# A 32x128 score product issued as four 32x32 products in a two-branch attention kernel

## The chip, the cores and the metric

The kernel runs on one core of a Trainium2 chip. The metric is the device time of one execution in microseconds (us). The other seven cores are idle.

## What is computed

Two attention blocks over their own inputs, 2048 tokens, 1024 features, 32 heads of 32 features each; their outputs stand side by side. All data is bf16.

```
# A: full softmax attention
q, k, v = split(x @ wqkv)                       # 32 heads of 32
p = softmax(q @ k.T * 32**-0.5)                 # 2048 x 2048 per head
a = (p @ v) @ wo
# B: four segments of 512 tokens, causal inside a segment, with a memory M, z carried over
for s in range(4):
    p = softmax(qs @ ks.T * scale + mask)       # 512 x 512 per head
    a_dot = p @ vs
    a_mem = (phi(qs) @ M) / (phi(qs) @ z + 1e-6)
    o[s] = g * a_mem + (1 - g) * a_dot
    M += phi(ks).T @ vs;  z += sum(phi(ks))
b = o @ wo
out = concat(a, b, -1)
```

## The kernel before

Every step is recorded as an operation of one engine (class `Prog`, `op`), with the tiles that it reads and writes, a planned duration and a key. `schedule` then runs a list scheduler once, while the program is built, and fixes the order of the operations on each engine; `emit` writes that order out with the semaphore waits that the dependencies ask for. So the order on TensorE is written into the program, and each engine works through its own list in that order. The planned duration of a score set is `w / 2400.0 + 0.012` (L917); `SWITCH = 0.10` is planned where the shape of TensorE's tiles changes.

Scores are made transposed: 128 keys on the partitions, queries along the columns. A *set* (`plan_set`, L871) is four tiles of 128 keys by 512 columns, one for each of four heads. A head has 32 features, so a score product has 32 rows of contraction and 128 columns of stationary operand (the keys). The four heads of a set stand at rows 0, 32, 64 and 96 of the array and write to four different PSUM banks. For block A a tile has two pieces of 256 columns, so a set is eight products of 32 rows by 128 columns with 256 moving columns (L915). For block B a set has two or three pieces of 256 or 128 columns, eight or twelve products (`tiles_att_B`, L826). There are 512 sets of A (4096 products) and 80 of B (768 products).

PSUM has eight banks. Six of them make three slots of two banks (`SLOT_BANKS`, L23); a set takes two slots. Bank 6 is for the projections and other jobs, bank 7 for the attention output. ScalarE works one slot at a time: `plan_exp` (L963, activation at L994) takes the exponential of 128x1024 scores into the ring `P`. Of some sets of A one head's tile is not exponentiated by ScalarE but approximated by a cubic (`plan_cube`, L939): VectorE reads the scores (`Y`, L952), GpSimd works on them (`Z`, L955 and L956), and VectorE finishes (`Pc`, L957); ScalarE's activation of that slot is then 128x512.

TensorE has, beside the score sets, the products `P @ V` (L1090) and the row sums with a matrix of ones (L1097), and all projections by `mm4` (L551; the product is L556): four products of 128 rows by 32 columns side by side, writing to the four quarters of the partitions of one bank. So TensorE alternates between tiles of 128x32 and, for the score sets, tiles of 32x128. A score set waits until ScalarE has emptied the slots that it writes; an activation waits for the whole set, since only the last product of a set raises the semaphore.

The keys and queries of the score products lie in `KQ_A` and `KQ_B`, made by `proj_job` and copied out of PSUM by VectorE (L1248).

Of the kernel before, what the change touches and what calls it, by code (L numbers as in the profile page):

```python
# [72 lines left out]
def holds(rs, *tag):  # L73
    for r in rs:
        assert r.tag == tag, (r.tag, tag)
# [448 lines left out]
class _Kernel:  # L524
# [346 lines left out]
    def plan_set(self, take, T):  # L871
        w = take[0]["w"]
        slots = [(self.slot_n + k) % 3 for k in range(2)]
        n = self.slot_n + 1
        self.slot_n += 2
        banks = SLOT_BANKS[slots[0]] + SLOT_BANKS[slots[1]]
        kind = take[0]["kind"]
        cube = kind == "A" and take[0]["set"][3] in self.cubed(take[0]["unit"], take[0]["part"])
        bufs = [self.p_next(2 - (cube and not k)) for k in range(2)]
        for k, t in enumerate(take):  # L880
            t["n"] = n
            self.sets.setdefault(t["set"], []).append(t)
            if cube and not k:
                continue
            i = bufs[k // 2] + (0 if cube and k == 1 else k % 2)
            t["P"] = (self.Pt, i, self.r_P[i])

        def f(key):
            res = [self.bank[x] for x in banks]
            mms = []  # L890
            rd = []
            for p in range(len(take[0]["pieces"])):
                for b, t in enumerate(take):
                    kt, q, nq, off, g = t["pieces"][p]
                    h = t["h"]
                    rows = slice(32 * h, 32 * h + 32)
                    if kind == "A":
                        sl = g % 2
                        holds([r for x in self.r_KQA[sl] for r in x], "KQ", g)
                        kap = self.KQA[rows, sl, 0, P * kt:P * kt + P]  # L900
                        qap = self.KQA[rows, sl, 1, q:q + nq]
                        rd += [self.r_KQA[sl][0][kt // 4], self.r_KQA[sl][1][q // 512]]
                    else:
                        holds(self.r_KQB[g], "KQ", take[0]["s"], g)
                        kap = self.KQB[rows, g, 0, P * kt:P * kt + P]
                        qap = self.KQB[rows, g, 1, q:q + nq]
                        rd += [self.r_KQB[g][0], self.r_KQB[g][1]]
                    out = self.ps[:, 512 * banks[b] + off:512 * banks[b] + off + nq]
                    mms.append((out, kap, qap, h, p == 0))
            rd = list(dict.fromkeys(rd))  # L910

            def mm(e):
                ins = None
                for out, kap, qap, h, st in mms:
                    ins = e.matmul(out, kap, qap, start=st, stop=True, tile_position=(32 * h, 0), skip_group_check=True)  # L915
                return ins
            o = self.pe(mm, w / 2400.0 + 0.012, key - 1.5, rd, res, mode="row")  # L917
            o.urgent = True
            o.heat = 1.0
        self.item(T, f)  # L920
        T0 = T
        fix = self.fixes.pop(n - 1, None)
        if cube:
            self.fixes[n - 1 + CARRY - CARRY % 2] = self.plan_cube(take[0], banks[0], T)
        for k in range(2):
            lo = int(cube and not k)
            self.plan_exp(take[2 * k:2 * k + 2], slots[k], bufs[k], T, lo, fix if k == CARRY % 2 else None)
            T += (2 - lo) * w / 1200.0 + EXP_FIXED
        u = take[0]["unit"]
        self.st.setdefault(u, T0)  # L930
        self.en[u] = T
        if kind == "B":
            if take[0]["set"][3] == 2:
                self.st["B", u[1], u[2] + 1] = T0
            self.en["B", u[1], u[2] + 1] = T
        self.rounds.append((take, T, cube))
        return T
# [967 lines left out]
```

## Time and profile before

| | |
|---|---|
| times, three runs | 1124.29, 1128.17, 1129.32 us; median 1128.17 |
| the profiled execution, first to last instruction | 1128.2 us, equal to the median run; nothing is shown beside it |
| instructions | 67476, of them 31412 matmuls and 31412 weight loads |
| TensorE (PE) | busy 1045.6 us, 93% |
| ScalarE (ACT) | busy 1071.5 us, 95% |
| VectorE (DVE), GpSimd (POOL) | 744.9 us, 66%; 677.5 us, 60% |
| granted TensorE clock, mean | 0.996 |

How to read it: busy time is the time in which at least one instruction of the engine is under way. Matmuls are recorded with a modelled end, and several run beside each other in different tiles of the array, so the busy share of PE says how much of the time it had something, not how much of the array was used. In rows, `32*128 32x256` is a product with 32 rows and 128 columns of the array and a moving operand of 32 partitions by 256 columns. PEld is the weight load that goes ahead of each product. The chain is followed back from the last instruction, at each step to what released it or to the instruction before it on its engine.

### The profile page before, as it was taken

The page shows a single profiled execution, that of the slowest core. Times are in us where ns is not written, and L with a number is a line of the kernel's source. Part 1 is how long each engine was busy: PE and PEld are TensorE (multiplying, and loading weights), DVE is VectorE, ACT ScalarE, POOL GpSimd, SP SyncE. Part 2 cuts the span into 40 slices and gives each one's busy share as a digit, 9 for nine tenths or more (in the row PEclk, how much of TensorE's full clock was granted, in tenths as well). Part 3 has the DMA queues.
Part 4 walks back from the last instruction along what each step waited for, and adds up shares of the span by engine and source line. Part 5 has one row for each costly group of instructions (what it writes and reads, how often), then busy time and mean ns, then how long its engine had stood idle before and what let it go on. Part 6 is the DMA issues. An engine that isn't in the chain of part 4 may idle for free.

```text
span 1128.2 us, 67476 instructions
## 1 busy us (share of the span) xinstructions
PE 1045.6 (93%) x31412; PEld 724.2 (64%) x31412; DVE 744.9 (66%) x1566; ACT 1071.5 (95%) x1224; POOL 677.5 (60%) x653
## 2 busy tenths in 40 slices
PE   8989999999999988998999898988999889999998
PEld 4667666667666655666666566766667556657775
DVE  3345667756665588777865888687745868775444
ACT  4989999999999999999999999999999979999997
POOL 2215576756576576856565786775755758665431
PEclk9999999999999999999999999999999989999999
DMA  9032350005223240033241330133040640022101
GB/s 203 7 85 46 83 130 15 16 19 121 54 56 88 64 104 13 16 72 63 65 90 59 82 59 11 33 87 85 27 101 28 200 111 3 23 69 76 39 23 54
DMA packets 171145, 72.77 MB, mean 64 GB/s; under 512 B 134768, under 2 KB 169072, under 8 KB 170864
## 3 DMA queue, kind: packets, MB, share of 16 engines
q1 hardware_dynamic: 168496, 67.66, 24.8%
q8 instruction: 246, 4.03, 1.5%
q10 hardware_dynamic: 2368, 0.79, 0.3%
q14 instruction: 35, 0.29, 0.1%
HBM read 45.23 MB, written 11.67 MB: 50 GB/s over the span
## 4 chain that ended last, share of the span: by engine, by line
ACT 48%; PE 35%; DVE 8%; issue 4%; POOL 2%; SPq 1%; DMA 1%; ACTq 0%; DVEq 0%; POOLq 0%
ACT P L994 47%; PE ps L556 17%; PE ps L915 7%; PE ps L1090 5%; PE ps L1097 5%; DVE PKQ_B L1546 1%; DVE Y L952 1%; DVE Pc L957 1%; SPq L1232 1%; PE ps L1495 1%; POOL Z L955 1%; ACT PKQ_B L1541 1%; DVE T L1115 1%; POOL Z L956 1%; DVE rc L1127 1%
## 5 line engine op out<-in xcount | busy, mean ns | idle before, releaser
L994 ACT ACTIVATE P<-ps 128x1024 bf16<-128x1024 f32 (+1 forms) x1176 | 1043.1, 1076 | 35.0 <-PE ps L1097 12.9
L1097 PE MATMUL ps<-P,onesb 128*32 128x256 bf16 (+1 forms) x4628 | 297.7, 271 | 1.0 <-issue 1.0
L955 POOL TENSOR_SCALAR Z<-Y 128x512 f32<-128x512 f32 x118 | 182.2, 1544 | 158.1 <-DVE Y L952 157.5
L1090 PE MATMUL ps<-P,V_A 128*32 128x256 bf16 x3860 | 254.9, 275 | 6.1 <-ACT P L994 2.1
L915 PE MATMUL ps<-KQ_A 32*128 32x256 bf16 x4096 | 205.2, 273 | 28.7 <-ACT P L994 18.9
L956 POOL TENSOR_TENSOR Z<-Z,Y 128x512 f32<-128x512 f32 x118 | 153.1, 1297 | 4.3
L915 PEld LDWEIGHTS ps<-KQ_A 32*128 32x128 bf16 x4096 | 61.9, 92 | 141.5 <-ACT P L994 100.9
L556 PE MATMUL ps<-xT_B,W_B 128*32 128x256 bf16 x4096 | 139.5, 275 | 6.1 <-issue 1.9
L556 PE MATMUL ps<-xT_A,W_A 128*32 128x256 bf16 (+1 forms) x3968 | 138.4, 277 | 5.3 <-DMA xT_A<-in_A_x_dram 1.6
L1097 PEld LDWEIGHTS ps<-P,onesb 128*32 128x32 bf16 x4628 | 130.3, 97 | 16.5 <-issue 12.1
L1014 POOL TENSOR_SCALAR_AFFINE_SELECT P<-P 128x768 bf16<-128x768 bf16 (+1 forms) x96 | 78.6, 823 | 90.7 <-ACT P L994 86.8
L1090 PEld LDWEIGHTS ps<-P,V_A 128*32 128x32 bf16 x3860 | 109.2, 96 | 32.3 <-issue 15.9
L952 DVE TENSOR_SCALAR Y<-ps 128x512 f32<-128x512 f32 x118 | 80.9, 686 | 72.3 <-PE ps L915 71.1
L1266 POOL TENSOR_TENSOR sqA<-KQ_A 128x512 bf16<-128x512 bf16 x61 | 66.6, 1094 | 96.9 <-DVE KQ_A L1248 57.2
L556 PEld LDWEIGHTS ps<-xT_B,W_B 128*32 128x32 bf16 x4096 | 100.5, 97 | 31.3 <-issue 24.1
L556 PEld LDWEIGHTS ps<-xT_A,W_A 128*32 128x32 bf16 x3968 | 97.5, 96 | 31.6 <-issue 17.0
L957 DVE SCALAR_TENSOR_TENSOR Pc<-Z,Y 128x512 bf16<-128x512 f32 x118 | 103.3, 876 | 18.9 <-POOL Z L956 18.5
L1266 POOL TENSOR_TENSOR sqB<-KQ_B 128x512 bf16<-128x512 bf16 x64 | 69.9, 1095 | 56.6 <-DVE KQ_B L1248 40.8
L1115 DVE STREAM_TRANSPOSE T<-ps 128x256 f32<-128x256 f32 (+1 forms) x148 | 71.9, 486 | 22.9 <-PE ps L1097 17.1
L1248 DVE CAST KQ_A<-ps 128x512 bf16<-128x512 f32 x60 | 41.2, 687 | 54.0 <-PE ps L556 53.7
L556 PE MATMUL ps<-Wv_B,xT_B 128*32 128x256 bf16 x2048 | 69.8, 274 | 4.8 <-DVE V_B L1248 1.4
L1129 DVE STREAM_TRANSPOSE T<-rc 128x256 f32<-128x256 f32 (+1 forms) x152 | 72.1, 478 | 2.5
(104 smaller groups left out, 1405.8 us busy)
## 6 DMA issues: line engine op xcount, KB each, us to landing
Wv_B<-in_B_wv_dram SPq DMA_DIRECT2D x32, 256.0 KB, 3.3
W_B<-in_B_wk_dram SPq DMA_DIRECT2D x32, 256.0 KB, 3.2
W_B<-in_B_wq_dram SPq DMA_DIRECT2D x32, 256.0 KB, 4.5
Wo_B<-in_B_wo_dram SPq DMA_DIRECT2D x32, 256.0 KB, 3.3
out_dram<-outsb SPq DMA_DIRECT2D x56, 128.0 KB, 1.8
W_A<-in_A_wqkv_dram SPq DMA_DIRECT2D x14, 256.0 KB, 3.6
ot_a_scratch<-OTst SPq DMA_DIRECT2D x50, 64.0 KB, 2.2
xT_A<-ot_a_scratch SPq DMA_DIRECT2D x6, 512.0 KB, 6.7
```

The lines of the kernel that those rows point to most:

```text
L556: ins = e.matmul(out[r], w[:, r], x, start=start, stop=stop, tile_position=(0, 32 * t), skip_group_check=True)
L915: ins = e.matmul(out, kap, qap, start=st, stop=True, tile_position=(32 * h, 0), skip_group_check=True)
L952: o = self.dve(lambda e: e.tensor_scalar(Y[:, :], src, KAPPA * SCALE, -KAPPA * ROOT, ALU.mult, ALU.add), 512, key - 9.0, [self.bank[bank]] ...
L955: self.pool(lambda e: e.tensor_scalar(Z[:, :], Y[:, :], CUBE_A, None, ALU.add), 512, key - BCK, [rY], [rZ], rate=0.38)
L956: self.pool(lambda e: e.tensor_tensor(Z[:, :], Z[:, :], Y[:, :], ALU.mult), 512, key - BCK, [rY, rZ], [rZ], rate=0.435)
L957: last.append(self.dve(lambda e: e.scalar_tensor_tensor(out=dst, in0=Z[:, :], scalar=CUBE_B, in1=Y[:, :], op0=ALU.add, op1=ALU.mult), 512, ...
L994: a = self.act(guarded if early else lambda e: e.activation(dst, src, ACT.Exp, scale=SCALE), cols, key, rd, wr, fixed=EXP_FIXED)
L1014: self.pool(lambda e: e.affine_select(v, v, pattern=pat, compare_op=ALU.is_ge, fill=0.0, base=0, channel_multiplier=-1), 2 * nd * P, key + ...
L1090: ins = e.matmul(self.ps[32 * h:32 * h + 32, 512 * obk + q0:512 * obk + q0 + nq], v, p, start=first, stop=last, tile_position=(0, 32 * h), ...
L1097: ins = e.matmul(self.ps[32 * h:32 * h + 32, lcol + q0:lcol + q0 + nq], self.onesb[:, 0:32], p, start=False, stop=last, tile_position=(0, ...
L1115: self.dve(lambda e: e.transpose(T2[:, 0:n], src), n, nk, rsrc, [r2], fixed=0.17)
L1266: self.pool(lambda e: e.tensor_tensor(sq[:, :], src, src, ALU.mult), 512, key, [rsrc], [rs], rate=0.5)
```

## The change

In `plan_set`, each score product of 32 rows by 128 columns (one head, 128 keys) is replaced by four products of 32 rows by 32 columns. They take the same 32 rows of the array and the four quarters of its columns; each has a quarter of the keys as stationary operand, the same queries as moving operand, and writes a quarter of the partitions of the same bank. The four stand directly behind each other, and the heads follow each other as before. A set of eight products becomes 32, one of twelve becomes 48; each has a weight load of its own.

```diff
             def mm(e):
                 ins = None
                 for out, kap, qap, h, st in mms:
-                    ins = e.matmul(out, kap, qap, start=st, stop=True, tile_position=(32 * h, 0), skip_group_check=True)
+                    for j in range(4):
+                        r = slice(32 * j, 32 * j + 32)
+                        ins = e.matmul(out[r], kap[:, r], qap, start=st, stop=True, tile_position=(32 * h, 32 * j), skip_group_check=True)
                 return ins
             o = self.pe(mm, w / 2400.0 + 0.012, key - 1.5, rd, res, mode="row")
```

The planned duration of a set is left as it is, so the order of the operations on every engine is the same as before; only each set has four times as many instructions. The semaphore is still raised by the last product of the set alone.

## The prediction

> **What bounds the kernel now.** I read the page first: busy shares, then the chain that ended last, then the group of the activations.
>
> ```profile
> span 1128.2 us, 67476 instructions
> ...
> PE 1045.6 (93%) x31412; PEld 724.2 (64%) x31412; DVE 744.9 (66%) x1566; ACT 1071.5 (95%) x1224; POOL 677.5 (60%) x653
> ...
> q8 instruction: 246, 4.03, 1.5%
> ...
> ACT 48%; PE 35%; DVE 8%; issue 4%; POOL 2%; SPq 1%; DMA 1%; ACTq 0%; DVEq 0%; POOLq 0%
> ...
> L994 ACT ACTIVATE P<-ps 128x1024 bf16<-128x1024 f32 (+1 forms) x1176 | 1043.1, 1076 | 35.0 <-PE ps L1097 12.9
> ```
>
> Two engines bound the kernel together. ACT is busy 95% of the span and waits only 35.0 us ahead of its exponentials; PE is busy 93%, so it has nothing under way for 1128.2 - 1045.6 = 82.6 us in all. The chain runs through ACT for 48% and through PE for 35%: it changes from one to the other, and time added to PE counts in the stretches where PE carries it. So the next view is the chain in order of time, its sum by line and a piece of a stretch that PE carries; then the timeline of that stretch on both engines.
>
> ```profile
> by line: ACT P L994 47.1%; PE ps L556 17.4%; PE ps L915 7.1%; PE ps L1090 5.0%; PE ps L1097 4.5%; issue 4.2%; DVE PKQ_B L1546 1.1%; DVE Y L952 1.0%; DVE Pc L957 1.0%; SPq L1232 0.9%; PE ps L1495 0.9%; POOL Z L955 0.7%; ACT PKQ_B L1541 0.7%;
> ...
> 340.49 0.11 PE ps L1097 x4
> 340.60 0.33 PE ps L915 x8
> 340.93 1.53 PE ps L556 x52
> 342.46 0.33 PE ps L915 x8
> ```
>
> ```profile
> 345.19 5.42 ACT L994 ACTIVATE P<-ps 128x1024 bf16<-128x1024 f32 x6
> ```
>
> ```profile
> 346.90 0.28 PE L1097 MATMUL ps<-P,onesb 128*32 128x256 bf16 x4
> 347.12 0.40 PE L915 MATMUL ps<-KQ_A 32*128 32x256 bf16 x8
> 347.45 0.29 PE L1090 MATMUL ps<-P,V_A 128*32 128x256 bf16 x4
> 347.57 0.28 PE L1097 MATMUL ps<-P,onesb 128*32 128x256 bf16 x4
> ```
>
> In this stretch PE goes from a set (L915) to other products and to the next set without a pause, while ACT also runs without a pause (six activations in one piece). Neither has room: that is the place where a longer set costs time. A set takes 0.33 us of the chain; L915 has 7.1% of 1128.2, 80.1 us, so 80.1 / 0.33 = 243 sets lie on the chain.
>
> **How many sets there are.** The groups by shape give the products that the change touches.
>
> ```profile
> L915 PE MATMUL ps<-KQ_A 32*128 32x256 bf16 x4096 | 205.2, 273 | 28.7 <-ACT P L994 18.9 <-DVE Y L952 3.4 <-issue 2.0
> L915 PE MATMUL ps<-KQ_B 32*128 32x256 bf16 x512 | 27.9, 271 | 1.3 <-ACT P L994 1.2
> L915 PE MATMUL ps<-KQ_B 32*128 32x128 bf16 x256 | 9.3, 219 | 0.9 <-ACT P L994 0.6
> ```
>
> These are 4864 products in 4096/8 = 512 sets of A and 80 of B: 592 sets. Of the 592, 243 are on the chain and 349 beside it. After the change there are 19456 products with as many weight loads: 14592 more of each.
>
> **What one set costs, now and then.** No product of 32x32 tiles is in this trace, so its cost comes from the nearest rows: one set looked at closely, once cut after its first four products, once whole, with its weight loads, and the durations of a single product of that kind (minimum, median, maximum).
>
> ```profile
> 400.97 0.12 PEld L915 LDWEIGHTS ps<-KQ_B 32*128 32x128 bf16 x8 [0.23 <-ACT P L994]
> ```
>
> ```profile
> 400.98 0.29 PE L915 MATMUL ps<-KQ_B 32*128 32x256 bf16 x4
> ...
> 400.98 0.40 PE L915 MATMUL ps<-KQ_B 32*128 32x256 bf16 x8
> ```
>
> ```profile
> L915 PEld LDWEIGHTS ps<-KQ_B x768: 90/93/94, 155.7 to 1005.3; 32*128 32x128 bf16 x192
> L915 PE MATMUL ps<-KQ_B x768: 214/268/278, 155.7 to 1005.3; 32*128 32x256 bf16 x128, 32*128 32x128 bf16 x64
> ```
>
> Four products take 0.29 us with one alone at 0.278: all four start within 0.012 us, 4 ns apart, and run beside each other in four tiles of the array. The whole set takes 0.40 with one at 0.268: the last product starts 0.13 us after the first, one stream of 256 columns (0.11, the step of the chain's `L1097 x4`) after its forerunner. The eight loads take 0.12 with one at 0.09, so they too start 4 ns apart, and the second four go ahead while the first four products stream.
>
> After the change the first piece has 16 products in 16 tiles, no two of which have the same rows and the same columns, or the same destination; the second piece has them again. I take the 4 ns step: 15 steps instead of 3 in each piece, so the last product of a piece starts 12 x 4 = 48 ns later. The second piece begins when the first tile is free, 0.12 us after the start as now: its 16 loads go from 0.06 to 0.12 us. So the set grows once, by 0.048 us, and its last start goes from 0.13 to 0.18. Streaming (two times 0.11) does not grow, because a product still streams 256 columns.
>
> This cost has two bounds. The upper one is from the densest long run of small products, 32 products 128 columns wide, in fours:
>
> ```profile
> 416.99 0.62 PE L556 MATMUL ps<-V_B,PKt_B 128*32 128x128 bf16 x32
> 417.43 0.28 PE L1090 MATMUL ps<-P,V_A 128*32 128x256 bf16 x4
> ```
>
> 32 products in 0.44 us is 13.8 ns each, the fastest at which this trace shows so many loads and products sustained: a set of 32 would have its last start at 31 x 13.8 = 0.43 instead of 0.13 us, 0.30 more. The lower bound is below nothing: of 346.90 to 347.12 (0.22) only 0.11 is streaming, and of 347.12 to 347.45 (0.33) 0.13 + 0.11 is; so the change of tile shape costs 0.11 us ahead of a set and 0.09 behind it. If going from 128x32 to 32x32 tiles needs no such pause, the set gets 0.20 - 0.048 = 0.15 us shorter. I take 0.048: the 4 ns steps belong to this very operation, and the 13.8 ns are four products per stream of 128 columns (0.055 us), so the stream and not the supply may set them. The pause I keep, since the tile's row count still changes.
>
> Here a rule of the Trainium skill speaks against the 4 ns. "TensorE: Matmul & The Clock Gate", section "Wait — 56ns, not 53.3ns?", says that starts of matmuls are never closer than about 25 ns, however small they are. By it the last of 32 products would start at 0.78 us, 0.65 later than now, 592 x 0.65 = 385 us, and with PE's 82.6 us of free time used up about 1430 us. The rows above disagree for products in different tiles: 4 ns, and 13.8 ns over 32. It has no chance of its own; a slow supply is rival 1.
>
> **The sum.** On the chain: 243 x 0.048 = 11.7 us. The 349 sets beside it would add 16.8 more if all came onto it; I count none, because there PE waits for ACT: L915 has 28.7 us of idle time ahead of it in the group above. That is the cover; if it is gone, the cost is 28.4 us. The exponential of a set waits for its last product, 0.048 later; where ACT carries the chain the set is ready ahead of it. VectorE's read of the cubic's tile (L952) also waits for the whole set; it moves by the same 0.048 and returns the slot that much later. Nothing is reordered and no wait is added; on PE's list everything behind a set moves by 0.048. The 29184 more instructions are fetched by queue q8: 4.03 MB for the old 62824, so 64 bytes each and 1.87 MB more, from 1.5% to 2.2% of the DMA engines; hidden beside the other transfers, and if fetches came late it would show as rival 1.
>
> 1128.2 + 11.7 = 1139.9, so 1140. The profiled execution is the median run (1128.17), so nothing is corrected between them.
>
> **The rivals.**
> 1. *The products cannot be supplied every 4 ns.* TensorE's list grows from 62824 to 92008 instructions, one every 12 ns over the whole span, and the rows show no such rate over a long time. At 13.8 ns a product, 592 x 0.30 = 178 us, less at most the 82.6 us in which PE is free: 95 us more, 1224 us. A step between 4 and 13.8 ns gives a time between; I count two thirds of this case under 1205. For it: nothing here shows 32 products within 0.2 us. Against it: twelve loads and products in about 0.03 us at 400.97.
> 2. *Tiles of one row group wait for each other.* A load for the second quarter would wait until the product in the first, in the same 32 rows, has streamed: three waits of 0.11 us for each of four heads and two pieces, 2.6 us a set, 592 x 2.6 = 1560 us, some 2700 us in all. Against it, with the same 128 rows for load and running product:
>
> ```profile
> 401.43 0.11 PEld L1090 LDWEIGHTS ps<-P,V_B 128*32 128x32 bf16 x4
> ```
>
> ```profile
> 401.43 0.28 PE L1097 MATMUL ps<-P,onesb 128*32 128x256 bf16 x4
> ```
>
> The loads start as those products start. "TensorE: Matmul & The Clock Gate", section "Part 3: Packing small matmuls — row/col tiling", says that a load overlaps a running matmul only if their row groups differ; the trace disagrees with that for 128x32 tiles, and no run here shows it for 32x32.
> 3. *It gets faster: no pause at the change of tile shape.* Each set gets 0.15 us shorter; from then on ACT decides, and the gain ends at its waits for PE. Of its 35.0 us of idle time, those for L1097 and L915 go:
>
> ```profile
> L994 ACT ACTIVATE P<-ps 128x1024 bf16<-128x1024 f32 x1058 | 1007.2, 1120 | 32.7 <-PE ps L1097 12.9 <-PE ps L556 8.3 <-PE ps L915 7.6
> ```
>
> 12.9 + 7.6 = 20.5 us, so 1108 us. It decides as soon as the saving at the two pauses is over 0.048 us. For it: both neighbours now have tiles 32 columns wide. Against it: the rows per tile still differ.
> 4. *The 0.048 us is hidden.* PE's waits ahead of the sets (28.7 us) take up what is added everywhere, since a stretch that PE carries ends in one: 1128 to 1133.
>
> That the change does not do what it says is excluded by the order of instructions: each set has 32 products where there were eight, and all else stands as before.
>
> **How the numbers follow.** The forecast (a start every 4 ns, pause kept, chain sets pay) has 0.55; rival 1 0.17, rival 2 0.04, rival 3 0.10, rival 4 0.14. A measurement tells a difference of some 0.5% (5.6 us) from no change. Faster is rival 3: 0.10; same is rival 4: 0.14; slower are the others: 0.76. The range goes from 1126 (rival 4, with the 2 us by which the runs differ) to 1205; outside are rivals 2 and 3 and a third of rival 1, 0.20. The forecast's own range is 1134 to 1157 (1128.2 + 28.4).
>
> **What would show it.** Right: in the changed trace a set has 32 products with starts 4 ns apart, its last start 0.18 us after its first, and takes 0.38 us on the chain; PE's share of the chain grows; the pauses stay at 0.11 and 0.09; ACT's idle time ahead of L994 grows by some 10 us. Wrong: a last start beyond 0.25 us (rival 1), starts 0.1 us apart (rival 2), a step of 0.11 from the last products before a set to the set (rival 3), or the same chain with sets of 0.38 us and no later end (rival 4).

## The result: 1403 us, a quarter slower

| | before | after |
|---|---|---|
| median of four runs, us | 1128.68 (1124.29 to 1129.32) | 1403.46 (1400.3 to 1412.28) |
| ratio, 95% interval | 1 | 1.2468 (1.2423 to 1.2514) |
| span of the profiled execution, us | 1128.2 | 1410.6 (its time 1412.28) |
| TensorE weight loads and products | 62824 | 92008 |

The forecast was 1140 us, the range 1126 to 1205. The direction was right, the size was wrong by a factor of more than twenty.

The page of the changed kernel has these lines for the ones shown of before: busy shares, the queue of the instructions, the chain, and the activations.

```profile
span 1410.6 us, 96660 instructions
...
PE 1149.5 (81%) x46004; PEld 796.7 (56%) x46004; DVE 724.6 (51%) x1566; ACT 1107.7 (79%) x1224; POOL 681.4 (48%) x653
...
q8 instruction: 360, 5.90, 1.7%
...
PE 70%; issue 15%; ACT 7%; DVE 5%; SPq 1%; DMA 0%; POOL 0%; ACTq 0%; DVEq 0%
...
L996 ACT ACTIVATE P<-ps 128x1024 bf16<-128x1024 f32 (+1 forms) x1176 | 1074.9, 982 | 279.9 <-PE ps L917 228.9
```

ACT now waits 279.9 us ahead of its exponentials, not 35.0, and mostly for score sets. But PE did not become busy: its share fell from 93% to 81%, and "issue" (time in which PE waited for nothing that the profile shows) went from 4% to 15% of the chain. So PE is the bound, and for 15% of the chain it stands still without a semaphore to wait for.

A stretch of the chain shows where, first pieces of it and then the same set on the timeline of PE:

```profile
310.28 0.37 PE ps L917 x32
...
311.86 0.33 PE ps L917 x29
312.19 2.10 issue
314.28 0.35 PE ps L917 x19
314.63 1.42 PE ps L556 x45
```

```profile
311.86 0.33 PE L917 MATMUL ps<-KQ_B 32*32 32x128 bf16 x29
314.28 0.35 PE L917 MATMUL ps<-KQ_B 32*32 32x128 bf16 x19 [2.10 <-issue]
```

The set at 310.28 costs 0.37 us on the chain, as forecast (0.38). The next set on the chain, at 311.86, has 48 products; it stops after 29 of them, for 2.1 us, and then goes on at the old pace. PE was not slowed while it worked; it stood. That it had no instructions is the suspicion that the next count tests.

That can be counted. I numbered all records of PE and PEld (loads, products, semaphore waits) in the order of their starts and added up the times from one start to the next ("gaps") by the number modulo 256. In the changed kernel, the gap ahead of number 193 has 288.7 us in all, the median of the 256 positions 4.3 us. In the kernel before the same position has 14.7 us, the median also 4.3. The difference at that one position, 274.0 us, is nearly as large as the 282.4 us between the two spans. (It is a sum by position and not by cause: the longer sets add to the other positions too, while the score sets' waits for ACT fell from 138.2 to 89.8 us.) A packet of queue q8 has 5.90 MB / 360 = 16.4 KB, 256 instructions of 64 bytes: the position is the border between two fetched blocks. The trace ties the two together: 255 of the 360 borders have a gap of over 0.5 us, 266.8 us in all, and at every one of them the next instruction starts 1.2 to 1.7 us after a packet of q8 has landed. No packet of q8 starts before the one ahead of it has ended. Over the span there is one block in 1410.6 / 360 = 3.9 us; the starts of two packets are never under 3.2 us apart, and the median is 3.7.

So I formed theory F: TensorE's instructions come in blocks of 256, and a block cannot come sooner than about 3.4 to 3.7 us after the one before; a list with too many instructions per time is bound by that, whatever the instructions do. Its rivals are these: S, the 32x32 tiles (or the added products as such) are slow; D, each instruction takes a fixed time in the sequencer, without blocks.

### The profile page after: what moved, and what is told of

Read it like the earlier page. It is cut to its first block, busy times and chain, and to the rows that moved or that the text cites. A ratio compares the mean times of both kernels' runs of the same rounds, so it can differ in the third digit from the quotient of the medians.

```text
span 1410.6 us, 96660 instructions
## 1 busy us (share of the span) xinstructions
PE 1149.5 (81%) x46004; PEld 796.7 (56%) x46004; DVE 724.6 (51%) x1566; ACT 1107.7 (79%) x1224; POOL 681.4 (48%) x653
## 4 chain that ended last, share of the span: by engine, by line
PE 70%; issue 15%; ACT 7%; DVE 5%; SPq 1%; DMA 0%; POOL 0%; ACTq 0%; DVEq 0%
PE ps L556 34%; PE ps L917 17%; PE ps L1092 10%; PE ps L1099 8%; ACT P L996 7%; PE ps L1497 1%; DVE T L1117 1%; DVE OT_B L1569 1%; SPq L1234 1%; DVE Y L954 1%; DVE KQ_A L1250 0%; DMA xT_A<-in_A_x_dram 0%; ACT P L983 0%; DVE cols L1284 0%; DVE T L1120 0%
## 5 line engine op out<-in xcount | busy, mean ns | idle before, releaser
L996 ACT ACTIVATE P<-ps 128x1024 bf16<-128x1024 f32 (+1 forms) x1176 | 1074.9, 982 | 279.9 <-PE ps L917 228.9
L1099 PE MATMUL ps<-P,onesb 128*32 128x256 bf16 (+1 forms) x4628 | 312.1, 273 | 19.0 <-issue 18.8
L917 PE MATMUL ps<-KQ_A 32*32 32x256 bf16 x16384 | 255.1, 276 | 82.4 <-issue 65.5
L1092 PE MATMUL ps<-P,V_A 128*32 128x256 bf16 x3860 | 267.4, 276 | 23.2 <-issue 19.0
L917 PEld LDWEIGHTS ps<-KQ_A 32*32 32x32 bf16 x16384 | 109.7, 88 | 211.9 <-issue 130.5
L556 PE MATMUL ps<-xT_A,W_A 128*32 128x256 bf16 (+1 forms) x3968 | 149.3, 282 | 23.3 <-issue 16.4
L1099 PEld LDWEIGHTS ps<-P,onesb 128*32 128x32 bf16 x4628 | 141.3, 97 | 43.6 <-issue 37.6
L959 DVE SCALAR_TENSOR_TENSOR Pc<-Z,Y 128x512 bf16<-128x512 f32 x118 | 88.7, 752 | 11.1 <-POOL Z L958 9.2
L1250 DVE CAST KQ_B<-ps 128x512 bf16<-128x512 f32 x64 | 44.1, 689 | 92.9 <-PE ps L556 92.5
L1250 DVE CAST outsb<-ps 128x512 bf16<-128x512 f32 x56 | 38.6, 689 | 92.3 <-PE ps L556 67.1
```

Of the source, the lines that this page charges most:

```text
L556: ins = e.matmul(out[r], w[:, r], x, start=start, stop=stop, tile_position=(0, 32 * t), skip_group_check=True)
L917: ins = e.matmul(out[r], kap[:, r], qap, start=st, stop=True, tile_position=(32 * h, 32 * j), skip_group_check=True)
L959: last.append(self.dve(lambda e: e.scalar_tensor_tensor(out=dst, in0=Z[:, :], scalar=CUBE_B, in1=Y[:, :], op0=ALU.add, op1=ALU.mult), 512, ...
L996: a = self.act(guarded if early else lambda e: e.activation(dst, src, ACT.Exp, scale=SCALE), cols, key, rd, wr, fixed=EXP_FIXED)
L1092: ins = e.matmul(self.ps[32 * h:32 * h + 32, 512 * obk + q0:512 * obk + q0 + nq], v, p, start=first, stop=last, tile_position=(0, 32 * h), ...
L1099: ins = e.matmul(self.ps[32 * h:32 * h + 32, lcol + q0:lcol + q0 + nq], self.onesb[:, 0:32], p, start=False, stop=last, tile_position=(0, ...
```

## Experiments

**e1: the supply of instructions by itself.** A program of its own, run once, without the kernel's work. The first two small sections differ in the shape of the tiles and the number of columns (shortened from the program):

```diff
+for j in range(4):                        # 128x32 tiles, 64 columns
+    e.matmul(ps[r, 0:64], w[:, r], x[:, 0:64], ..., tile_position=(0, 32 * j))
...
+for h in range(4):                        # 32x32 tiles, 256 columns
+    for j in range(4):
+        e.matmul(ps[r, 512 * h:512 * h + 256], w[k, r], x[k, 0:256], ..., tile_position=(32 * h, 32 * j))
```

> The kernel's work is left out; TensorE alone runs five sections: 1024 full products 256 columns wide, 2048 products of 128x32 tiles 64 columns wide (array time some 7 ns each, 15 us in all), 512 full ones, 2048 products of 32x32 tiles 256 columns wide (again some 7 ns each, 15 us), 512 full ones, and the 128x32 section again with DMA loads beside it. Theory F (blocks of 256 instructions of TensorE arrive no faster than one in 3.4 to 3.7 us): both quiet sections of small products, 4096 instructions or 16 blocks each, take 50 to 60 us whatever the tile shape, less what was fetched ahead, with bursts a few ns apart and stalls of 1 us and more every 256 instructions; with DMA beside it, longer, 60 us or more. The full sections run at 0.107 us a product. Theory D (a fixed time per instruction, 13 to 14 ns): the same total of 55 us, but evenly spread steps without stalls. Theory S (32x32 tiles as such are slow): the 128x32 section takes 15 us, the 32x32 section several times as long.

The busy time of each engine in the three small sections (128x32 quiet, 32x32 quiet, 128x32 with DMA loads; each row has the stretch, its length, the busy time of PE, PEld and POOL, the granted TensorE clock, the busy share of the DMA engines and their GB/s), and a piece of the timeline of the first two and of the third:

```profile
116.60:171.80 55.20, 28.40 (x2050) 26.28 (x2048) 0.00 (x0) 0.56 0.02 4
229.00:284.30 55.30, 30.01 (x2048) 24.53 (x2048) 0.00 (x0) 0.56 0.02 4
341.70:410.30 68.60, 28.36 (x2049) 26.28 (x2048) 0.00 (x0) 0.55 0.85 187
```

```profile
142.34 1.90 PE L28 MATMUL ps<-x,w 128*32 128x64 bf16 x128 [1.56 <-issue]
145.80 1.90 PE L28 MATMUL ps<-x,w 128*32 128x64 bf16 x128 [1.56 <-issue]
...
152.71 1.90 PE L28 MATMUL ps<-x,w 128*32 128x64 bf16 x128 [1.56 <-issue]
156.43 1.90 PE L28 MATMUL ps<-x,w 128*32 128x64 bf16 x128 [1.83 <-issue]
```

```profile
251.20 1.99 PE L38 MATMUL ps<-x,w 32*32 32x256 bf16 x128 [1.74 <-issue]
254.66 1.99 PE L38 MATMUL ps<-x,w 32*32 32x256 bf16 x128 [1.46 <-issue]
```

```profile
368.50 1.90 PE L28 MATMUL ps<-x,w 128*32 128x64 bf16 x128 [1.83 <-issue]
373.62 1.90 PE L28 MATMUL ps<-x,w 128*32 128x64 bf16 x128 [3.22 <-issue]
```

Both quiet sections take 55.2 us for 4096 instructions, whatever the tile: 128 products with their 128 loads run in one go, then PE stands for 1.5 to 1.8 us, and the next 128 mostly begin 3.45 or 3.73 us after the first. S would have made the sections differ, D would show no bursts; both fall. Over the section that is 13.5 ns an instruction, but its first block and three quarters had been fetched ahead. From the end of one stall to the end of the next it is 3.6 us on average in both sections, 14.1 ns an instruction, 28 ns a load and product together. The packets of q8 divide these 3.6 us: the next fetch starts 1.1 us after the border is passed, the packet takes 1.1 us, and the first instruction starts 1.4 us after it has landed. With transfers at 187 GB/s beside it the same section takes 68.6 us, 4.5 us from stall to stall on average. The packet (1.0 us) and the time after it (1.4) are as before; the fetch starts 1.9 us after the border instead of 1.1 (medians). What holds its start up is not shown. The first section of full products (one load and product in 111 ns) showed no stall; in the small section after it 447 instructions went through before the first. These 447 are the last 191 of the block in use and one whole block of 256, so no more than one whole block was held ahead. The Trainium skill, "Runtime: NRT & Kernel Launch", section "Instruction fetch mechanics", says that an engine's instructions come in 16 KiB blocks of 256, the next one fetched through a DMA queue while the current one is executed; the trace agrees (16.4 KB a packet, stalls every 256). It also says that the fetch is hidden because instructions are issued more slowly than blocks arrive; for TensorE these runs disagree (1.5 us and more of standing at each block in e1).

**e2: the number of instructions without the shape.** The score products stay 32x128; small ones ahead of them bring each set to the number after the change.

```diff
+                for _ in range(3 * len(mms) // 4):
+                    for out, kap, qap, h, st in mms[:4]:
+                        e.matmul(out[:, 0:8], kap, qap[:, 0:8], start=True, stop=True, tile_position=(32 * h, 0), skip_group_check=True)
                 for out, kap, qap, h, st in mms:
                     ins = e.matmul(out, kap, qap, start=st, ...)
```

> Score products are 32x128 as in the kernel before; ahead of each set stand products 8 columns wide, of the same 32x128 shape and to the same place, which are overwritten, so that each set has as many instructions as after the change (32 or 48 products). Theory F: the number of instructions alone decides, 1380 to 1430 us, with stalls at every 256th instruction. Theory S (32x32 tiles are slow): only the added products' own time, some 0.15 us a set, on the 243 sets of the chain: 1140 to 1170 us.

1414.47 us, ratio 1.2558 (1.251 to 1.2605). With no 32x32 product at all the kernel is as slow as after the change, and position 193 has 234.5 us. The page shows the same queue and the same stall:

```profile
q8 instruction: 360, 5.90, 1.7%
...
PE 77%; issue 12%; ACT 5%; DVE 5%; SPq 1%; POOL 0%; DMA 0%; DVEq 0%; ACTq 0%
```

**e3 and e4: fewer added products.** In e3 a place has two products of 32x64, in e4 only the first piece of a set is split in four. Both are shown against the changed kernel, shortened.

```diff
-                    for j in range(4):
-                        r = slice(32 * j, 32 * j + 32)
+                    for j in range(2):                        # e3, with tile_position=(32 * h, 64 * j)
+                        r = slice(64 * j, 64 * j + 64)
...
+                    n = 4 if st else 1                        # e4
+                    for j in range(n):
+                        r = slice(P // n * j, P // n * j + P // n)
```

> Two products of 32x64 at each place in place of four of 32x32: TensorE's list has 72552 instructions, 284 blocks. Theory F: 284 blocks of 3.7 us are 1051 us, under the time before, so only dense stretches stall: 1130 to 1165 us. Theory S or any cost per added product: a third of the loss, 1220 us.

> Only the first piece of each set is split in four: 77032 instructions, 301 blocks. Theory F: 301 blocks of 3.7 us are 1114 us, just under the time before, so many stretches stall: 1150 to 1200 us. A cost per added product: 49% of the loss, 1262 us.

e3: 1172.59 us, ratio 1.0402 (1.0372 to 1.0431), a little above what F expected and well under a third of the loss. Position 193 has 59.7 us, 45.0 more than before; the span is 43.0 us longer. So 284 blocks already stall in dense stretches, although their number times 3.7 us is under the time.

e4: 1225.57 us, ratio 1.0886 (1.0839 to 1.0932), above what F expected and under the other. Position 193 has 60.4 us, 45.7 more than before, but the span is 95.6 longer. Half of the loss is something else: the set itself got longer. On PE's timeline

```profile
603.91 0.55 PE L918 MATMUL ps<-KQ_B 32*32 32x256 bf16 x20
604.39 0.24 PE L1093 MATMUL ps<-P,V_B 128*32 128x128 bf16 x4
```

from the set's first product to what follows it are 0.48 us, 0.15 more than the 0.33 before and 0.11 more than the 0.37 of a whole split set. The 0.11 lie between the pieces, where e4 changes from 32x32 to 32x128 tiles; I had not expected this pause. 592 x 0.15 = 89 us on PE, part of which falls into PE's free time; that this is the other 50 us is argued, not measured apart.

**e5 and e6: fewer instructions elsewhere.** The projections' four products of 128x32 side by side become one of 128x128, in the kernel before (e5, the control) and in the changed one (e6).

```diff
-        for t in range(4):
-            r = slice(32 * t, 32 * t + 32)
-            ins = e.matmul(out[r], w[:, r], x, ..., tile_position=(0, 32 * t), ...)
-        return ins
+        return e.matmul(out, w, x, start=start, stop=stop, skip_group_check=True)
```

> Control: score products as before; each group of four 128x32 projection products side by side is one product of 128x128 with the same 256 or 512 moving columns: 24486 instructions less (38338, 150 blocks), the same streaming time, but 591 more changes of tile shape of some 0.1 us on TensorE. Theory F alone gains little (the kernel before loses some 10 us at block boundaries), the changes of shape cost up to 59 us less what TensorE's free time covers: 1115 to 1190 us.

> The changed kernel with the same one-product projections: 67522 instructions, 264 blocks, near the kernel before. Theory F: 264 blocks of 3.7 us are 977 us, so nearly all of the 275 us comes back; within 30 us of the control, 1130 to 1210 us, with few stalls at every 256th instruction. Any theory in which the added score products cost time by themselves: 275 us above the control, 1390 to 1460 us.

e5: 1145.78 us, ratio 1.0168 (1.0144 to 1.0192): I put this down to the added changes of tile shape, which was not measured apart. e6: 1183.09 us, ratio 1.05 (1.0474 to 1.0526). All the 32x32 products are there, yet 220 of the 275 us came back. Between e6 and its control are 37.6 us of span; 13.4 of them are at position 193 (19.3 against 5.9), and 592 sets of 0.04 us more (medians 0.370 and 0.329) are 24 us. So the two together give the difference if every set counts in full, and the cost of the longer set stands here almost alone; PE carries 76% of e6's chain, and "issue" has fallen to 3%. F expected at most 30 between them; 37 is a little more.

```profile
PE 76%; ACT 10%; DVE 8%; issue 3%; POOL 2%; DMA 1%; DVEq 0%; POOLq 0%; ACTq 0%
```

```profile
600.28 0.37 PE ps L914 x32
...
602.28 0.36 PE ps L914 x31
602.65 0.56 issue
603.21 0.26 PE ps L914
```

```profile
603.17 0.33 PE ps L912 x8
```

These are the chain of e6 by engine, pieces of it in order of time and, last, a piece of the chain of e5: 0.37 against 0.33, and in e6 a remaining stall inside a set.

**e7 and e8: fewer instructions without another change of tile shape.** One product replaces four only where everything between two score sets on TensorE's list can be written so; e7 is the kernel before, e8 the changed one (the edit shortened).

```diff
+        self.whole, seg = set(), []
+        for o in [*queue["PE"], None]:
+            if o is not None and o.mode != "row":
+                seg.append(o)
+                continue
+            if all(x.mode == "full" or "mm4" in x.fn.__code__.co_names for x in seg):
+                self.whole |= set(seg)
+            seg = []
...
+            self.one = o in self.whole
...
+        if self.pg.one:                                       # the operation is in whole
+            return e.matmul(out, w, x, start=start, stop=stop, skip_group_check=True)
```

> The kernel before, with one 128x128 product in place of four 128x32 ones only where everything between two score sets can be so written: 6510 instructions less (56314, 220 blocks) and no change of tile shape more. Theory F: the kernel before loses some 10 us at block boundaries, part of which comes back: 1115 to 1126 us. If instructions cost nothing there: 1128 us.

> The changed kernel with the same replacement: 85498 instructions, 334 blocks. Theory F: 334 blocks at the 3.9 us that a block takes in the changed kernel are 1303 us; 1280 to 1330 us, so some 100 us come back, although only products beside the score sets were joined. A cost of the 32x32 products themselves: 1395 to 1405 us.

e8: 1326.95 us, ratio 1.1764 (1.1725 to 1.1804). 7% fewer instructions, none of them taken from the score sets, bring 76 us back; position 193 has 204.9 us, 190.2 more than before, and the span is 194.4 us longer. e7: 1124.0 us, ratio 0.9974 (0.996 to 0.9988), so a little faster than the kernel before, in the range that F gave. Position 193 fell from 14.7 to 8.1 us, 6.6 us, and the comparison shows some 3 (medians 1126.66 and 1124.00); the joined products are another difference, so that the gain is the fetch's is not shown.

```profile
span 1119.2 us, 60966 instructions
...
q8 instruction: 221, 3.62, 1.4%
```

Over the runs, position 193 against the lengthening of the span (us, to the kernel before; e6 to e5):

| kernel | blocks | gaps at 193, more by | span, more by |
|---|---|---|---|
| after | 360.7 | 274.0 | 282.4 |
| e2 | 360.7 | 219.8 | 281.2 |
| e8 | 335.3 | 190.2 | 194.4 |
| e4 | 302.2 | 45.7 | 95.6 |
| e3 | 284.7 | 45.0 | 43.0 |
| e6 | 265.1 | 13.4 | 37.6 |

The two columns need not agree: what makes a set longer stands in the second alone, and where PE had free time it costs less. In e2 the rest is put down to the added products, which stand 0.17 us ahead of a set on PE's timeline and make it 0.15 us longer from its first start to what follows (0.48 against 0.33); that was not measured apart.

## Why the prediction was wrong

What bounds the kernel (ACT and PE together, 243 sets on the chain) held as far as it went. The cost of one set was right, as a set without a stall shows on PE's timeline of the changed kernel:

```profile
600.47 0.44 PE L917 MATMUL ps<-KQ_A 32*32 32x256 bf16 x32 [0.57 <-ACT P L996]
600.84 0.40 PE L556 MATMUL ps<-PKQ_B,Zb 128*32 128x512 bf16 x4
...
601.82 0.28 PE L1092 MATMUL ps<-P,V_A 128*32 128x256 bf16 x4
602.03 0.33 PE L917 MATMUL ps<-KQ_A 32*32 32x256 bf16 x16
```

0.44 us less one product's 0.27 puts the last start 0.17 us after the first (forecast 0.18); within a piece the single starts are 3 to 4 ns apart. A set takes 0.37 us to what follows it (forecast 0.38), so the pause at the change of tile shape stayed: 0.09 us behind this set and 0.10 ahead of the next (601.82 to 602.03, of which 0.11 is streaming; that set is cut by the end of the window). e6 against e5 puts this cost at 24 of 37.6 us, inside the 11.7 to 28.4 that the sum gave; there PE carries 66 to 76% of the chain instead of 35%, so sets that I counted as free can come onto it. Rivals 2 (tiles of one row group wait), 3 (no pause) and 4 (hidden) did not happen: the starts are 3 to 4 ns apart, the pauses are there, and the kernel is slower.

Two steps failed, both about the supply of instructions.

The first is the sentence that the 29184 additional instructions are "hidden beside the other transfers". I priced the fetch by its bytes, 2.2% of the DMA engines. It is not bound by bytes: no packet of q8 starts before the last has ended, and in e1 3.6 us pass from border to border, of which the packet's own time is 1.1. The term that I put at nothing cost 274.0 us at the borders. The page had the numbers to see it: 1128.2 us over 246 packets is a block every 4.6 us on average, and 360 packets at the same pace would be 1651 us. Whether 4.6 was the kernel's own pace or near the limit was the question to ask. Had I looked at the packets of q8 then, the shortest time between the starts of two fetches in the trace of before, 3.3 us, and the median, 4.3, would have suggested that the margin is small.

The second is the upper bound. I called 13.8 ns a product "the fastest at which this trace shows so many loads and products sustained" and took it as the worst case. The 32 products of that row are 64 instructions, a quarter of a block that was already there. A burst from the stock bounds nothing that has to last: e1 has 28 ns for a load and product sustained, and inside a set of the changed kernel 16 of them start within 0.05 us. So rival 1 named the right place, and its argument ("one every 12 ns over the whole span, and the rows show no such rate over a long time") was the right one: 12 ns an instruction was asked for, 14.1 is what e1 had with the DMA engines quiet. But its price, 1224 us, was built on the burst, so of the cases that had a chance only rival 2 led beyond it. At the rate of e1, an estimate is 92008 x 14.1 ns = 1297 us, and with transfers beside the fetch (4.5 us a block, 17.6 ns an instruction) 1619; the kernel lies between. The sign that I named for rival 1, a last start beyond 0.25 us, looked for slow steps inside every set; the stalls fall wherever a block ends, and 413 of the 512 sets of A have no step of over 0.3 us.

The rule of the Trainium skill that starts are never closer than some 25 ns ("TensorE: Matmul & The Clock Gate", section "Wait — 56ns, not 53.3ns?") gave 1430 us, near the measured time. That is a coincidence: inside the sets the starts are 3 to 4 ns apart, and the time is lost mainly in 255 gaps of 0.5 to 3.8 us.

## What to carry to other kernels

Count the instructions of an engine against time, not only their durations: here TensorE's list came at 256 instructions in 3.6 us with the DMA engines quiet and in 4.5 beside 187 GB/s (e1), and in 3.9 over the changed kernel. The kernel before, at 4.6, had little room: 15% more instructions (e3) already cost 4%, however cheap each one is. Look for the stall that has no releaser ("issue") and number the records modulo 256; and when a bound is taken from a burst, ask whether the burst is longer than what was in stock. Where four products side by side can be one of the same streaming time without a further change of tile shape, joining them was a small gain here (e7), and with one a loss (e5).

## What the runs showed of the hardware that was not expected

The fetch is sensitive to data traffic: 55.2 us became 68.6 us with 187 GB/s beside it (e1). The granted TensorE clock fell to 0.56 on average in the starved sections of e1, where PE is idle half of the time. The blocks came no slower for it: 3.6 us there, and a median of 3.7 us between two fetches in the changed kernel at 0.985. Against 0.996 before, the clock can be no more than a small part of this loss. And the pause at a change of tile shape also comes between 32x32 and 32x128 tiles inside a set (e4).
